# Weight conversion in a float64-weight MoE kernel: rounding the high part before the low word is added, and keeping the sum in the raw tile

## The chip, the cores and the metric

One core of one Trainium2 chip. The metric is the device time of one launch in microseconds (us). TensorE does the matmuls; VectorE, ScalarE and GpSimd do element-wise work on 128 partitions; SyncE (SP) only issues DMAs.

## The reference

Three stages in a row. The kernel's inputs are those of `setup_inputs`; the MoE weights arrive as 64-bit floats (each an `int64` bit pattern of two 32-bit words), everything else as float32.

```
attention (4 batches, 8 heads, 576 positions, head 64):
    scores = q k^T / 8 * Dmat,  Dmat = gamma_h ** (i - j) for i >= j, else 0
    x = scores @ v                                  -> 2304 tokens x 512
first MoE:   h = x @ w_in (512 x 2048);  g = (a0 + a1 h + a2 h^2 + a3 h^3)
                 / (1 + |b0||h| + |b1| h^2 + 1e-6);   x = g @ w_out
second MoE:  xn = x / sqrt(mean(x^2) + 1e-6) * rms_g
             out = (silu(xn @ w_gate) * (xn @ w_val)) @ w_out2    (512 x 1536)
```

## The kernel before

Attention runs in chunks of 128 positions (20 steps) with a running state. Both MoEs work in tiles of 384 tokens, six tiles each, features on the partitions. To keep float32 accuracy at the speed of the `fp32r` matmul format, each operand is split into a high part (rounded to fp32r) and a low part (the remainder rounded to fp32r), and each product is three matmuls: high x high, high x low, low x high. So every weight block of 128 x 512 values has to become a tile `w[:, 0]` (high) and `w[:, 1]` (low), and since the weights arrive as 64-bit floats, each must first be made a float32.

That conversion is the class `Weights`. A block goes through these steps; `hi` and `lo` are the high and the low 32-bit words of the 64-bit values, each every second word of the raw tile:

- `load` (L129): SP loads 512 KB into a `raw` tile.
- `begin`: ScalarE reads `hi` into a work tile `ft` with a scale (L141) and turns `lo` into an integer carry, in place (L142). VectorE shifts and masks `ft` (L143) and puts the sign in from `hi` (L147). GpSimd adds `lo` to `ft` as integers (L150): `ft` is then the float32 value. The next load is asked for.
- `finish`: ScalarE rounds `ft` to the high part (L156), and the engine that is passed in (VectorE or GpSimd) subtracts it from `ft` and writes the low part (L157).
- `step` does one `finish` and one `begin`, so a block is finished one step after it was begun.

`raw` has three tiles for the first MoE's weights and two for the second's; `ft` has two in both. A load needs a raw tile whose readers are done; L141 needs an `ft` tile whose readers are done.

Two instances exist. `wa` converts the 32 blocks of the first MoE during attention and the first token tile (about the first 205 us). `wb` loads two blocks then, begins its first conversions in the last token tile of the first MoE, and does most of its 36 blocks (gate, value, out for each of 12 j) in the loop over j in which the second MoE's first two token tiles are worked side by side (about 545 to 700 us). Each j of this loop has two `m2_up` (24 matmuls each: gate into bank 4, value into bank 6) and two `m2_down` (9 matmuls each), and three `step_b`: one on VectorE and two on GpSimd. `step_b` wraps the step in `tc.issue_after(mark["el"])`: its ScalarE instructions are issued behind the latest SiLU (L441). After that the remaining four token tiles need no conversion.

The order of the instructions on each engine, and of the DMAs on SP's queue, is not the order of the source: a planner puts them in order by its own estimates of when each is ready, with the source order as priority, and inserts the semaphore waits. Each engine, and SP's queue, then works strictly in that order.

Of the kernel before, what the change touches and what calls it, by code (L numbers as in the profile page):

```python
# [7 lines left out]
F32 = mybir.dt.float32  # L8
# [3 lines left out]
ACTF = mybir.ActivationFunctionType  # L12
ALU = mybir.AluOpType
# [26 lines left out]
def retention_moe_kernel(  # L40
# [19 lines left out]
    act, dve, pool, pe, sp = nc.scalar, nc.vector, nc.gpsimd, nc.tensor, nc.sync  # L60
# [55 lines left out]
    class Weights:  # L116
# [17 lines left out]
        def begin(self):  # L134
            w = self.alloc(self.n1)
            self.n1 += 1
            raw = self.raw.pop(0)
            ft = self.ft_p.tile([128, 512], I32, tag="ft", name="ft")
            f = ft.bitcast(F32)
            hi, lo = raw[:, :, 1], raw[:, :, 0]  # L140
            act.activation(out=f, in_=hi.bitcast(F32), func=ACTF.Copy, scale=2.0 ** -112)  # L141
            act.activation(out=lo, in_=lo.bitcast(U32), func=ACTF.Copy, scale=2.0 ** -29)  # L142
            dve.tensor_scalar(  # L143
                out=ft, in0=ft, scalar1=3, scalar2=0x7FFFFFFF,
                op0=ALU.logical_shift_left, op1=ALU.bitwise_and,
            )
            dve.scalar_tensor_tensor(  # L147
                out=ft, in0=hi, scalar=-0x80000000, in1=ft, op0=ALU.bitwise_and, op1=ALU.bitwise_or
            )
            pool.tensor_tensor(out=ft, in0=ft, in1=lo, op=ALU.add)  # L150
            self.mid.append((w, f))
            self.load()

        def finish(self, eng):
            w, f = self.mid.pop(0)
            act.activation(out=w[:, 0], in_=f, func=ACTF.Copy)  # L156
            eng.tensor_tensor(out=w[:, 1], in0=f, in1=w[:, 0].bitcast(F32), op=ALU.subtract)  # L157
            self.got[self.order[self.n2]] = w
            self.n2 += 1
# [367 lines left out]
    for h in range(NH - 1, -1, -1):  # L527
        pool.tensor_tensor(
            out=dmk8[:, h], in0=dmk8[:, 0], in1=gi[:, h].to_broadcast([128, CH]), op=ALU.mult
# [241 lines left out]
```

## Time and profile before

| | us |
|---|---|
| median of 3 runs | 1014.8 |
| lowest, highest | 1012.92, 1021.29 |
| profiled execution | 1015.87 |
| its span, first to last instruction | 1014.1 |
| TensorE busy | 976.3 |
| VectorE, ScalarE, GpSimd busy | 576.0, 550.8, 419.5 |
| mean granted TensorE clock (1 is full) | 0.982 |

The difference between the profiled execution and its span, 1.8 us, lies around the first and the last instruction. A busy time is the union of an engine's instructions; instructions on one engine overlap a little at their ends. "SPq" is SP's queue of DMA issues.

### The profile page before, as it was taken

How to read it: one execution, taken by the hardware profiler on the slowest of the kernel's cores; microseconds unless marked ns; L12 is line 12 of the kernel's file. 1: busy time of each engine (PE TensorE's matmuls, PEld its weight loads, DVE VectorE, ACT ScalarE, POOL GpSimd, SP SyncE). 2: the span in 40 equal slices, each digit the busy share in tenths (PEclk: the TensorE clock that was granted, in tenths of full speed). 3: DMA queues.
4: the chain of work that ended last, by engine and by line, in shares of the span. 5: the costliest groups of instructions: out<-in, count | busy, mean ns of one | idle time of the engine just before them, and what ended most of it. 6: DMA issues, size and time to landing. Idle time of an engine off the chain costs nothing.

```text
span 1014.1 us, 14962 instructions
## 1 busy us (share of the span) xinstructions
PE 976.3 (96%) x5726; PEld 912.9 (90%) x5726; DVE 576.0 (57%) x972; ACT 550.8 (54%) x1076; POOL 419.5 (41%) x379
## 2 busy tenths in 40 slices
PE   8989899889999999999989999999999999999998
PEld 6878677889999999999989989889999999999997
DVE  4999999768668677686797664444211211212211
ACT  3777676587786877878878665555212112111111
POOL 4475676574564654746647545545001001000000
PEclk7999999999999999999999999999999999999999
DMA  7848676310100100101012243333200100000000
GB/s 266 268 139 262 211 236 204 102 57 32 32 1 32 32 1 32 32 32 32 21 53 90 91 154 119 110 124 96 72 1 16 48 1 16 32 1 1 32 1 32
DMA packets 37592, 78.91 MB, mean 78 GB/s; under 512 B 5904, under 2 KB 21392, under 8 KB 37520
## 3 DMA queue, kind: packets, MB, share of 16 engines
q1 hardware_dynamic: 36512, 77.61, 23.6%
q8 instruction: 45, 0.74, 0.3%
q10 hardware_dynamic: 1008, 0.34, 0.1%
q14 instruction: 27, 0.22, 0.1%
HBM read 64.57 MB, written 13.37 MB: 77 GB/s over the span
## 4 chain that ended last, share of the span: by engine, by line
PE 58%; DVE 10%; ACT 5%; POOL 5%; DMA 4%; issue 3%; POOLq 0%; DVEq 0%; ACTq 0%
PE bank L438 7%; PE bank L436 7%; PE bank L437 7%; PE bank L308 4%; PE bank L317 4%; PE bank L318 4%; PE bank L309 4%; PE bank L310 4%; PE bank L321 4%; PE bank L454 4%; PE bank L455 4%; PE bank L453 4%; DMA raw<-in_w_val_dram 3%; POOL ft L150 3%; DVE ft L147 2%
## 5 line engine op out<-in xcount | busy, mean ns | idle before, releaser
L438 PE MATMUL bank<-x,w 128*128 128x384 f32 x528 | 177.6, 336 | 1.7 <-POOL w L157 1.7
L436 PE MATMUL bank<-x,w 128*128 128x384 f32 x528 | 177.2, 336 | 1.8 <-DVE sg L442 1.8
L437 PE MATMUL bank<-x,w 128*128 128x384 f32 x528 | 177.0, 335 | 0.0
L442 DVE TENSOR_TENSOR sg<-sg,bank 128x384 f32<-128x384 f32 x72 | 39.8, 553 | 218.6 <-PE bank L438 218.3
L150 POOL TENSOR_TENSOR ft<-ft,raw 128x512 int32<-128x512 int32 x68 | 96.1, 1413 | 120.0 <-DVE ft L147 64.2
L308 PE MATMUL bank<-x,w 128*128 128x384 f32 x384 | 131.8, 344 | 5.9 <-DVE u L346 4.8
L344 POOL TENSOR_TENSOR q<-q,ah 128x384 f32<-128x384 f32 x96 | 101.9, 1063 | 81.2 <-ACT q L340 80.7
L318 PE MATMUL bank<-g,w 128*128 128x384 f32 x384 | 126.1, 343 | 6.1 <-DVE w L157 6.1
L310 PE MATMUL bank<-x,w 128*128 128x384 f32 x384 | 131.0, 341 | 0.9 <-POOL w L157 0.6
L309 PE MATMUL bank<-x,w 128*128 128x384 f32 x384 | 130.1, 339 | 1.3 <-DVE x L212 1.3
L317 PE MATMUL bank<-g,w 128*128 128x384 f32 x384 | 126.3, 344 | 3.3 <-ACT g L364 3.3
L365 POOL TENSOR_TENSOR g<-u,g 128x384 fp32r<-128x384 f32 x96 | 100.7, 1049 | 67.0 <-issue 34.5
L441 ACT ACTIVATE sg<-bank 128x384 f32<-128x384 f32 x72 | 35.3, 490 | 147.8 <-PE bank L438 147.8
L212 POOL TENSOR_TENSOR x<-xr,x 128x384 fp32r<-128x384 f32 x44 | 46.2, 1063 | 157.8 <-ACT x L211 157.6
L436 PEld LDWEIGHTS bank<-x,w 128*128 128x128 f32 x528 | 99.2, 188 | 5.4 <-DVE sg L442 2.1
L438 PEld LDWEIGHTS bank<-x,w 128*128 128x128 f32 x528 | 99.1, 188 | 3.1 <-POOL w L157 3.0
L437 PEld LDWEIGHTS bank<-x,w 128*128 128x128 f32 x528 | 99.1, 188 | 3.0 <-POOL x L212 0.3
L444 ACT ACTIVATE y<-sg 128x384 fp32r<-128x384 f32 x72 | 37.6, 522 | 104.4 <-DVE sg L442 104.3
L345 DVE TENSOR_TENSOR u<-u,bank 128x384 f32<-128x384 f32 x96 | 52.9, 551 | 59.4 <-ACT u L341 58.8
L321 PE MATMUL bank<-g,w 128*128 128x384 f32 x384 | 86.6, 339 | 0.0
L308 PEld LDWEIGHTS bank<-x,w 128*128 128x128 f32 x384 | 73.1, 191 | 8.8 <-DVE u L346 6.2
L318 PEld LDWEIGHTS bank<-g,w 128*128 128x128 f32 x384 | 72.5, 192 | 8.8 <-DVE w L157 7.5
(98 smaller groups left out, 2080.8 us busy)
## 6 DMA issues: line engine op xcount, KB each, us to landing
raw<-in_w_out_dram SPq DMA_DIRECT2D x28, 512.0 KB, 3.5
xb<-in_qkT_dram SPq DMA_DIRECT2D x19, 512.0 KB, 4.1
kv<-in_kv_dram SPq DMA_DIRECT2D x16, 512.0 KB, 4.4
raw<-in_w_in_dram SPq DMA_DIRECT2D x16, 512.0 KB, 4.5
raw<-in_w_gate_dram SPq DMA_DIRECT2D x12, 512.0 KB, 3.5
raw<-in_w_val_dram SPq DMA_DIRECT2D x12, 512.0 KB, 3.6
xn_d<-x SPq DMA_DIRECT2D x6, 768.0 KB, 3.8
xr<-xn_d SPq DMA_DIRECT2D x24, 192.0 KB, 2.5
```

The lines of the kernel that those rows point to most:

```text
L150: pool.tensor_tensor(out=ft, in0=ft, in1=lo, op=ALU.add)
L308: pe.matmul(out=h, lhsT=w[:, 0, ks], rhs=x[:, 0, k], start=(k == 0), stop=False)
L309: pe.matmul(out=h, lhsT=w[:, 0, ks], rhs=x[:, 1, k], start=False, stop=False)
L310: pe.matmul(out=h, lhsT=w[:, 1, ks], rhs=x[:, 0, k], start=False, stop=(k == KD - 1))
L317: pe.matmul(out=acc[m], lhsT=w[:, 0, ms], rhs=g[:, 0], start=(j == 0), stop=False)
L318: pe.matmul(out=acc[m], lhsT=w[:, 1, ms], rhs=g[:, 0], start=False, stop=False)
L321: pe.matmul(out=acc[m], lhsT=w[:, 0, ms], rhs=g[:, 1], start=False, stop=(j == J1 - 1))
L344: pool.tensor_tensor(out=q, in0=q, in1=ah, op=ALU.mult)
L365: pool.tensor_tensor(out=g[:, 1], in0=u, in1=g[:, 0].bitcast(F32), op=ALU.subtract)
L436: pe.matmul(out=t, lhsT=w[:, 0, ks], rhs=x[:, 0, k], start=(k == 0), stop=False)
L437: pe.matmul(out=t, lhsT=w[:, 0, ks], rhs=x[:, 1, k], start=False, stop=False)
L438: pe.matmul(out=t, lhsT=w[:, 1, ks], rhs=x[:, 0, k], start=False, stop=(k == KD - 1))
```

## The change

The ScalarE rounding of the high part moves from `finish` to `begin`, behind the line of the GpSimd sum, and reads `ft`, which no longer gets the low word's bits. The GpSimd sum goes to `lo`, every second word of the raw tile, and the subtraction in `finish` reads it from there. The high part is then the rounding of a value that lacks the low word's carry; the low part is taken against the full sum, so that high plus low still stands for the full value.

```diff
-            pool.tensor_tensor(out=ft, in0=ft, in1=lo, op=ALU.add)
-            self.mid.append((w, f))
+            pool.tensor_tensor(out=lo, in0=ft, in1=lo, op=ALU.add)
+            act.activation(out=w[:, 0], in_=f, func=ACTF.Copy)
+            self.mid.append((w, lo.bitcast(F32)))
             self.load()
 
         def finish(self, eng):
             w, f = self.mid.pop(0)
-            act.activation(out=w[:, 0], in_=f, func=ACTF.Copy)
             eng.tensor_tensor(out=w[:, 1], in0=f, in1=w[:, 0].bitcast(F32), op=ALU.subtract)
```

## Rows read from the trace of the kernel before

**Rows 1.** The page's first part: busy us, share of the span, instructions.

```profile
PE 976.3 (96%) x5726; PEld 912.9 (90%) x5726; DVE 576.0 (57%) x972; ACT 550.8 (54%) x1076; POOL 419.5 (41%) x379
```

**Rows 2.** Busy us (instructions) of PE, PEld, DVE, ACT, POOL in two stretches; clock, DMA.

```profile
40.00:160.00 120.00, 108.92 (x878) 92.29 (x877) 118.08 (x175) 85.66 (x166) 79.18 (x62) 0.97 0.68 217
...
600.00:700.00 100.00, 97.79 (x509) 90.00 (x508) 47.33 (x83) 53.63 (x100) 50.11 (x39) 1.00 0.35 111
```

**Rows 3.** Chain of waits, 598 to 634 us: start, us, what.

```profile
604.95 3.55 DMA raw<-in_w_val_dram
...
611.67 1.31 POOL ft L150
612.98 1.26 POOL w L157
...
614.27 0.68 ACT ft L141
...
616.73 1.42 POOL ft L150
```

**Rows 4.** Timeline of SP's queue: first and last of 15 raw issues; a value load.

```profile
81.54 0.33 SPq L129 DMA_DIRECT2D raw<-in_w_in_dram  x1
...
156.88 0.33 SPq L129 DMA_DIRECT2D raw<-in_w_in_dram  x1
...
684.89 0.33 SPq L129 DMA_DIRECT2D raw<-in_w_val_dram  x1
```

**Rows 5.** Timelines of GpSimd and VectorE, second conversion: start, us, instruction, idle before.

```profile
608.45 1.32 POOL L150 TENSOR_TENSOR ft<-ft,raw 128x512 int32<-128x512 int32 x1 [3.52 <-DVE ft L147]
...
666.35 2.54 POOL L157 TENSOR_TENSOR w<-ft,w 128x512 fp32r<-128x512 f32 x2
...
618.84 0.69 DVE L157 TENSOR_TENSOR w<-ft,w 128x512 fp32r<-128x512 f32 x1 [1.87 <-ACT w L156]
```

**Rows 6.** Timeline of TensorE: starts of up, down, next up; a wait.

```profile
608.94 0.33 PE L436 MATMUL bank<-x,w 128*128 128x384 f32 x1
...
613.13 0.39 PE L453 MATMUL bank<-w,y 128*128 128x512 f32 x1
...
615.21 0.33 PE L436 MATMUL bank<-x,w 128*128 128x384 f32 x1
...
667.69 0.44 PE L438 MATMUL bank<-x,w 128*128 128x384 f32 x1 [0.41 <-POOL w L157]
```

**Rows 7.** TensorE's waits, 560 to 720 us: total, times, longest.

```profile
PE bank L438 <- POOL w L157: 1.7, 3, 1.0
```

**Rows 8.** TensorE's waits, 0 to 215 us.

```profile
PE bank L318 <- DVE w L157: 6.1, 5, 2.0
...
PE bank L308 <- ACT w L156: 1.0, 1, 1.0
```

**Rows 9.** ScalarE's waits, 0 to 215 us.

```profile
ACT ft L141 <- DVE w L157: 17.8, 12, 3.7
```

**Rows 10.** Conversion lines over the span: ns minimum/median/maximum, first and last start.

```profile
L150 POOL TENSOR_TENSOR ft<-ft,raw x68: 1288/1320/1761, 17.9 to 696.6; 128x512 int32<-128x512 int32 x68
...
L156 ACT ACTIVATE w<-ft x64: 612/630/647, 19.2 to 679.6; 128x512 fp32r<-128x512 f32 x64
...
L157 DVE TENSOR_TENSOR w<-ft,w x37: 677/693/1784, 22.1 to 672.2; 128x512 fp32r<-128x512 f32 x37
L157 POOL TENSOR_TENSOR w<-ft,w x27: 1270/1298/1732, 37.3 to 680.7; 128x512 fp32r<-128x512 f32 x27
...
L147 DVE SCALAR_TENSOR_TENSOR ft<-raw,ft x68: 674/686/1687, 17.1 to 695.6; 128x512 int32<-128x512 int32 x68
...
L143 DVE TENSOR_SCALAR ft<-ft x68: 406/428/1467, 15.2 to 694.8; 128x512 int32<-128x512 int32 x68
```

**Rows 11.** Timelines of GpSimd and VectorE: one early weight's sum and subtraction.

```profile
137.88 1.62 POOL L150 TENSOR_TENSOR ft<-ft,raw 128x512 int32<-128x512 int32 x1 [2.43 <-DMA kv<-in_kv_dram]
...
141.68 1.48 DVE L157 TENSOR_TENSOR w<-ft,w 128x512 fp32r<-128x512 f32 x1
```

## The prediction

> **What bounds the kernel now.** I read the page's busy line first: TensorE is busy 96% of the span, nothing else above 57% [rows 1]. So only TensorE's gaps are for sale, and the change touches only the weight conversion. It runs in two stretches, which the windows separate [rows 2]. In 40 to 160 us (first MoE's weights, beside attention) VectorE is busy 118.08 of 120 us and sets the pace. In 600 to 700 us (second MoE's weights) VectorE, ScalarE and GpSimd are all about half busy, TensorE 97.79 of 100. The chain of waits there does not run through TensorE but round a ring of conversion steps [rows 3]: raw load issued at 604.95, GpSimd's sum for that weight over at 611.67 + 1.31 = 612.98, a GpSimd subtraction to 614.24, the ScalarE conversion of the next weight, which that subtraction released by freeing a ft tile, its sum to 618.15, then the next load. From the value load at 604.95 to that at 684.89 [rows 3, 4] there are six rounds of three weights (gate, value, out): 79.94 / 6 = 13.32 us a round. TensorE needs 2 x (615.21 - 608.94) = 12.54 us a round [rows 6]. So the ring is the slower by 0.78 us, TensorE eats a small lead, and then waits for the low part of a weight: three waits, 1.7 us [rows 7], one at 667.69 [rows 6], just behind the gate's subtraction (666.35 + 2.54 / 2 = 667.62) [rows 5].
>
> **The change, part by part.**
> (a) The ScalarE rounding moves from finish to begin and needs the VectorE bit operations, no longer GpSimd's sum. It runs beside the sum (0.63 us against 1.32 [rows 10]), so the subtraction can follow the sum at once. In its new place ScalarE may stand through the two VectorE operations (0.43 + 0.69 = 1.1 us at the medians [rows 10]) with the SiLU and the y rounding queued behind it. ScalarE is busy 53.63 of 100 us [rows 2] and TensorE's down projection gives 615.21 - 613.13 = 2.08 us [rows 6] between reading a bank and needing it again: cost nothing; without that cover, up to 1.1 us at each of two SiLUs a round, 13 us over six rounds.
> (b) The ft tile is freed by sum and rounding instead of by the subtraction. That removes ScalarE's waits for ft: 17.8 us in 12 waits in the first stretch [rows 9], and the link at 614.27 [rows 3].
> (c) The raw tile is now freed by the subtraction, not by the sum. With two raw tiles in the second stretch, that is the ring that is left. Load issue to end of sum takes 612.98 - 604.95 = 8.03 us [rows 3]. Behind it comes the subtraction: on GpSimd directly after the sum 1.29 us, on VectorE (one weight in three) 0.77 us with its start delay [rows 5, 10]. Three weights: 3 x 8.03 + 1.29 + 1.29 + 0.77 = 27.44 us, over two tiles 13.72 us a round. That is 0.40 above 13.32; six rounds, 2.4 us later at the end.
> (d) Against that, the subtractions come sooner after their sums. Now the gate's ends 614.24 - (608.45 + 1.32) = 4.47 us after its sum, because the value's sum is queued ahead of it on GpSimd; the value's 2.52; out's 619.53 - 618.15 = 1.38 [rows 3, 5]. After: 1.29, 1.29, 0.77. TensorE uses the value's low part 12 matmuls after the gate's, 12 x 0.175 = 2.1 us later (24 in 613.13 - 608.94 [rows 6]), at 669.8; it is ready at 668.89 [rows 5], 0.9 us early, and becomes 1.23 us earlier still. So TensorE can run 2.1 us closer to the conversion. Net of this stretch: 2.4 - 2.1 = +0.3 us.
> (e) Strides. VectorE's subtraction reads every second word: the bit operation that already does so takes 686 ns against 693 contiguous [rows 10], so nothing. On GpSimd a strided read shows as 1320 against 1298 [rows 10]: +0.02. No row shows GpSimd writing with a stride; the floor is 0 (its reads stay, so no gain), the far end its slowest sum, 1761 ns, 0.44 more [rows 10]. I take 0.02, as the strided read is the nearest row; the far end adds 3 x 0.44 / 2 = 0.66 a round, 4.0 us.
> (f) SP's queue: every raw load now waits for the subtraction. In the second stretch nothing but raw loads stands behind it. In the first, attention's loads and stores do. Raw loads there come every (156.88 - 81.54) / 14 = 5.38 us [rows 4], 16.1 us for three tiles; load to sum 8.03, sum to subtraction 143.16 - 139.50 = 3.66 [rows 11], together 11.7. With 4.4 us to spare this ring does not bind: nothing, at worst the few microseconds by which attention's loads slip.
> (g) First stretch: ScalarE's ft waits go, but VectorE has the same operations and no room, so TensorE's waits there (6.1 and 1.0 us behind the conversion [rows 8]) stay. Bounds: 0 to -7; I take 0, since 118.08 of 120 is nearer to full than anything else here.
>
> Sum: the profiled execution took 1015.87 us (span 1014.1 and 1.8 around it); + 0.3 gives 1016.2. That execution is 1.07 above the median of the runs, so on the median's scale **1015 us**, and 1010 to 1021 for this case with strides, ScalarE's queue and SP's.
>
> **A rule against it.** VectorE's shift takes 428 ns at the median but up to 1467, the bit merge 686 and up to 1687 [rows 10]: VectorE loses time when GpSimd runs beside it. The Trainium skill, "SBUF — State Buffer", section "Who interferes with whom", says that a VectorE operation in a two-port mode or with two SBUF inputs and a GpSimd operation that reads SBUF exclude each other for a whole instruction; the slow rows agree in kind. It makes the third rival.
>
> **Rivals.**
> B, the subtraction stays where it is in the engines' queues. The order comes from a planner, not from this page. If GpSimd keeps the value's sum ahead of the gate's subtraction, the raw tiles are held 4.47, 2.52 and 1.38 us past the sums: (3 x 8.03 + 8.37) / 2 = 16.2 us a round, six rounds 6 x 2.9 = 17 us: 1032, more if the weights before 604.95 suffer too. It decides as soon as the mean delay from sum to end of subtraction is above 1.9 us (15 us a round, 1% of the time over six). For: that is today's order, and a load's wait then holds all loads behind it. Against: the reason for the order, a rounding that comes late on ScalarE, goes away. Chance 0.16.
> C, the ft waits did cost: their release lets the rounding chain run ahead, TensorE's 6.1 + 1.0 us [rows 8] in the first stretch and 1.7 us [rows 7] in the second vanish: 1006. For: ScalarE's ft waits stand at nearly every weight. Against: VectorE's 118.08 of 120. Chance 0.13, the part past 1% of it 0.06.
> D, exclusion. With subtraction directly behind sum, GpSimd works 2.6 us in one piece, and the other tile's shift or merge is held once per weight for the length of a subtraction, 1.27 us: (27.44 + 3.81) / 2 = 15.6 a round, + 2.3 x 6 - 2.1 = 11.7: 1027. For: the slow rows. Against: the pair at 666.35 [rows 5] already is such a piece, and its toll lies in the 8.03. Chance 0.07.
> That the change does not do what it says (rounding and sum side by side) would need ScalarE to be full; with 53.63 of 100 it is not, and I give it no chance of its own.
>
> **How the numbers follow.** No change, 1015: 0.64. The range leaves out B and the far edge of C, 0.16 and a few hundredths: 1006 to 1029. One per cent, about 10 us, is what a measurement of this kernel can tell from none. Faster by more: 0.07. Slower by more: B and most of D, 0.21. Within: 0.72.
>
> **What would show it.** Loads issued at the end of a subtraction, on SP, instead of a sum: (c). Round length between value loads near 13.7: the forecast; above 15: B or D, told apart by GpSimd's order (sum, sum, subtraction in B) and by the shift's mean (D). ScalarE without ft waits before 160 us but VectorE still full and TensorE's 40 to 160 us unchanged: (g); TensorE clearly busier there: C. A sum well above 1.32 us at its minimum: (e) wrong. SiLU waiting behind the rounding, with TensorE waiting for a bank: (a) wrong.

## The result: 0.65% slower, within the forecast of no change

| | before | after |
|---|---|---|
| median, us (13 runs each) | 1014.85 | 1021.31 |
| lowest to highest, us | 1009.91 to 1021.29 | 1018.93 to 1027.91 |
| ratio after / before, 95% interval | | 1.0065 [1.0048, 1.0083] |
| profiled execution, us | 1015.87 | 1022.4 |
| its span, us; granted TensorE clock | 1014.1; 0.982 | 1020.6; 0.974 |

The time lies within the range (1006 to 1029), and the loss is under the 1% that the forecast called no change. It is a loss all the same, 6.5 us, where the sum of terms gave +0.3. In the changed kernel's lines L150 is the sum (now into `raw`), L151 the rounding and L157 the subtraction.

The page's busy line, against [rows 1]: TensorE is busy 3.4 us longer, VectorE and ScalarE slightly less, GpSimd 5.7 us longer.

```profile
PE 979.7 (96%) x5726; PEld 920.3 (90%) x5726; DVE 574.7 (56%) x972; ACT 549.2 (54%) x1076; POOL 425.2 (42%) x379
```

The two stretches of [rows 2] (same columns). From 600 to 700 us TensorE is now busy throughout, at a lower granted clock; from 40 to 160 us the trace has 51 fewer matmuls than before (827 against 878), at 0.95 instead of 0.97, and VectorE is still nearly full.

```profile
40.00:160.00 120.00, 106.90 (x827) 93.24 (x826) 116.17 (x167) 85.79 (x169) 80.48 (x60) 0.95 0.62 203
600.00:700.00 100.00, 100.00 (x515) 93.80 (x514) 50.19 (x89) 55.98 (x101) 53.53 (x39) 0.97 0.41 129
```

**The second conversion does what the change promises.** Timelines of SP, GpSimd and VectorE in its steady part (start, us, instruction, idle before), against [rows 3 to 5]:

```profile
615.35 0.33 SPq L129 DMA_DIRECT2D raw<-in_w_val_dram  x1
...
621.80 1.50 POOL L150 TENSOR_TENSOR raw<-ft,raw 128x512 int32<-128x512 int32 x1 [1.14 <-issue]
623.37 1.32 POOL L157 TENSOR_TENSOR w<-raw,w 128x512 fp32r<-128x512 f32 x1
626.18 1.51 POOL L150 TENSOR_TENSOR raw<-ft,raw 128x512 int32<-128x512 int32 x1 [1.49 <-DVE ft L147]
...
627.72 0.69 DVE L157 TENSOR_TENSOR w<-raw,w 128x512 fp32r<-128x512 f32 x1 [1.21 <-POOL raw L150]
...
690.55 0.33 SPq L129 DMA_DIRECT2D raw<-in_w_val_dram  x1
```

The subtraction follows its sum at once: the value's sum ends at 621.80 + 1.50 = 623.30, its subtraction at 624.69, and a load (the gate's) is issued at 624.72. From value load to value load there are again six rounds: (690.55 - 615.35) / 6 = 12.53 us a round, TensorE's own pace (12.54) and no longer the ring's (13.32). No TensorE wait for a low part is left; those of [rows 7] are gone. TensorE's waits from 545 to 720 us (total, times, longest) are others:

```profile
PE bank L436 <- ACT sg L441: 4.7, 2, 2.8
PE bank L436 <- DVE u L346: 0.7, 1, 0.7
```

**It pays at the switch to the second MoE.** ScalarE's timeline at those two waits:

```profile
551.34 0.63 ACT L151 ACTIVATE w<-ft 128x512 fp32r<-128x512 f32 x1 [0.33 <-DVE ft L147]
551.99 1.28 ACT L441 ACT_TABLE_LOAD   x1
553.28 0.49 ACT L441 ACTIVATE sg<-bank 128x384 f32<-128x384 f32 x1
...
594.67 0.66 ACT L141 ACTIVATE ft<-raw 128x512 f32<-128x512 f32 x1 [2.55 <-DMA raw<-in_w_out_dram]
...
596.90 0.63 ACT L151 ACTIVATE w<-ft 128x512 fp32r<-128x512 f32 x1 [0.99 <-DVE ft L147]
597.54 1.28 ACT L441 ACT_TABLE_LOAD   x1
598.84 0.49 ACT L441 ACTIVATE sg<-bank 128x384 f32<-128x384 f32 x1
```

A SiLU stands behind a rounding, which stands behind VectorE's merge, and at 594.67 behind a raw load that could be issued only after a subtraction. TensorE waits 1.91 us up to 553.83 and 2.76 us up to 599.38, and the granted clock drops at each wait, to the lower of its two levels for 3.4 and 6.8 us (windows, columns as in [rows 2]):

```profile
553.00:560.00 7.00, 6.17 (x26) 6.17 (x27) 2.85 (x4) 5.51 (x10) 7.00 (x7) 0.76 0.45 126
598.00:606.00 8.00, 6.62 (x22) 6.62 (x23) 5.03 (x9) 4.01 (x7) 3.27 (x3) 0.57 0.51 164
```

**Where the 6.5 us arise.** I set the same instructions of both traces side by side, after minus before. The 17th evaluation of the first MoE (about 204 us) starts 3.9 us late; the lag is 2.4 to 4.7 us for the next 20 evaluations and 3.7 us in most of those after them, to about 530 us; at the seventh SiLU (589.5 us before) it is 9.4, at the tenth 11.0; it falls back to 6.2 at the 24th, since the conversion now keeps up, and stays at 6.6. In these two executions, then, some 3.7 us belong to the first conversion and the rest to the switch less the gain. Two single executions do not size this; the experiments weigh the two halves with many runs.

### The profile page after: what moved, and what is told of

The parts are those of the page before. It is cut to its first block, busy times and chain, and to the rows that moved or that the text cites. A ratio compares the mean times of both kernels' runs of the same rounds, so it can differ in the third digit from the quotient of the medians.

```text
span 1020.6 us, 15004 instructions
## 1 busy us (share of the span) xinstructions
PE 979.7 (96%) x5726; PEld 920.3 (90%) x5726; DVE 574.7 (56%) x972; ACT 549.2 (54%) x1076; POOL 425.2 (42%) x379
## 3 DMA queue, kind: packets, MB, share of 16 engines
q10 hardware_dynamic: 1008, 0.34, 0.1%
## 4 chain that ended last, share of the span: by engine, by line
PE 70%; DVE 6%; ACT 3%; POOL 2%; DMA 2%; issue 2%; DVEq 0%; ACTq 0%; POOLq 0%
PE bank L436 9%; PE bank L438 9%; PE bank L437 9%; PE bank L308 5%; PE bank L321 5%; PE bank L317 5%; PE bank L310 5%; PE bank L318 5%; PE bank L309 5%; PE bank L454 5%; PE bank L455 5%; PE bank L453 5%; DMA raw<-in_w_val_dram 1%; DVE x L417 1%; POOL w L157 1%
## 5 line engine op out<-in xcount | busy, mean ns | idle before, releaser
L150 POOL TENSOR_TENSOR raw<-ft,raw 128x512 int32<-128x512 int32 x68 | 99.1, 1458 | 99.3 <-DVE ft L147 64.7
L436 PEld LDWEIGHTS bank<-x,w 128*128 128x128 f32 x528 | 100.5, 190 | 9.1 <-ACT sg L441 5.3
L437 PEld LDWEIGHTS bank<-x,w 128*128 128x128 f32 x528 | 100.3, 190 | 2.8
L438 PEld LDWEIGHTS bank<-x,w 128*128 128x128 f32 x528 | 100.1, 190 | 0.1
L308 PEld LDWEIGHTS bank<-x,w 128*128 128x128 f32 x384 | 74.2, 193 | 9.8 <-DVE u L346 7.4
L310 PEld LDWEIGHTS bank<-x,w 128*128 128x128 f32 x384 | 74.4, 194 | 4.7 <-DVE w L157 4.1
```

Of the source, the lines that this page charges most:

```text
L150: pool.tensor_tensor(out=lo, in0=ft, in1=lo, op=ALU.add)
L308: pe.matmul(out=h, lhsT=w[:, 0, ks], rhs=x[:, 0, k], start=(k == 0), stop=False)
L310: pe.matmul(out=h, lhsT=w[:, 1, ks], rhs=x[:, 0, k], start=False, stop=(k == KD - 1))
L436: pe.matmul(out=t, lhsT=w[:, 0, ks], rhs=x[:, 0, k], start=(k == 0), stop=False)
L437: pe.matmul(out=t, lhsT=w[:, 0, ks], rhs=x[:, 1, k], start=False, stop=False)
L438: pe.matmul(out=t, lhsT=w[:, 1, ks], rhs=x[:, 0, k], start=False, stop=(k == KD - 1))
```

## The experiments

All ratios are to the kernel before on the same chip, with 95% intervals. Each expectation names the theories as they stood when it was written.

### Which half of the change, and which part

The change in the first conversion alone (`if self.order is not order:` keeps the old code for `wb`), and in the second alone:

> The change in the first MoE's conversion alone; the second MoE's is as before. Theory T (the loss lies in two places: 3.7 us by the end of the first conversion, 2.8 us net at the switch to the second MoE): +3.7 us, ratio 1.0037, all of it there by 205 us, and nothing lost or won after it. Rival R (the ring of raw tiles: only two tiles are too few, three have slack): no loss, 1.000. Rival P (any new order by the planner costs or gives a few us, here and there): anything within 0.7%, and what the two half changes cost does not add up to the whole.

> The change in the second MoE's conversion alone. Theory T: +2.8 us, ratio 1.0028: TensorE waits some 4.7 us in two stalls behind the first SiLU and the seventh, each followed by a stretch at half clock, about 6 us lost by the seventh SiLU; then the conversion keeps up (rounds near 12.6 us, no wait for a low part) and 3 to 4 us come back. Rival R: rounds longer than 13.3 us and longer waits for low parts, all of the 6.5 us here, 1.0065. Rival P: not 1.0065 less what the other half costs.

Measured: first only 1021.35 us, 1.0062 [1.0041, 1.0082], the whole loss; second only 1014.25, 0.9988 [0.9968, 1.0008], nothing. Theory T's sizes (1.0037 and 1.0028) and rival R's (1.000 and 1.0065) both missed. The cut is clean: up to 500 us ScalarE, VectorE and GpSimd work in the changed kernel's order in the first kernel, and in the order of before in the second. The second's trace has the same waits at the switch (TensorE's waits, 540 to 720 us; L447 is its SiLU), but here without any time at the lower clock level (1.00 over this stretch):

```profile
PE bank L442 <- ACT sg L447: 4.8, 3, 2.4
```

Its seventh SiLU is 5.1 us late and its 24th 0.4 us early: the stall is real, and by the 24th it is made up for, as the conversion keeps up. So the loss is to be sought in the first conversion, where only waits for weights had been looked at.

The two ideas of the change, one at a time, in both conversions. Early rounding, with the sum back in `ft` (against the kernel before; the rounding in `finish` goes):

```diff
+            act.activation(out=w[:, 0], in_=f, func=ACTF.Copy)
             pool.tensor_tensor(out=ft, in0=ft, in1=lo, op=ALU.add)
```

> Both conversions: the rounding early (in begin, ahead of the sum), but the sum back in the ft tile, so that the sum waits for the rounding and the raw tile is free after the sum. Leaves out the low word in the high part as the change does. Theory T: the stall behind the first SiLU comes from the rounding's place and stays (1.9 us and about 1.7 us of half clock), the one behind the seventh comes from a raw load that waits for a subtraction and goes; the first conversion as before: ratio 1.002 to 1.004. Rival R: the raw tiles are free as before, so 1.000.

And the sum in the raw tile, with the rounding left in `finish` (against the changed kernel):

```diff
             pool.tensor_tensor(out=lo, in0=ft, in1=lo, op=ALU.add)
-            act.activation(out=w[:, 0], in_=f, func=ACTF.Copy)
-            self.mid.append((w, lo.bitcast(F32)))
+            self.mid.append((w, lo.bitcast(F32), f))
...
-            w, f = self.mid.pop(0)
+            w, f, f0 = self.mid.pop(0)
+            act.activation(out=w[:, 0], in_=f0, func=ACTF.Copy)
```

> Both conversions: the sum in the raw tile as in the change, but the rounding (of the value without the low word) back in finish, so it comes a step later. Theory T: no stall behind the first SiLU, but loads late: the first conversion's 3.7 us and a stall at the seventh SiLU stay: 1.003 to 1.006. Rival R: the raw tile is held even longer than in the change (the subtraction waits for the late rounding), rounds near 16 us, 15 us or more lost: above 1.012.

Measured: early rounding 1012.93 us, 0.9974 [0.9951, 0.9996]; sum in raw 1023.89, 1.0082 [1.0051, 1.0113]. The early rounding gains about 2.6 us; the sum's new place costs 8 to 9 us. Neither theory had these sizes: T expected 1.002 to 1.004 and 1.003 to 1.006, R 1.000 and above 1.012.

### What of the sum's new place

With the sum in `raw`, the subtraction no longer reads `ft`, so an `ft` tile comes free earlier. Laid side by side, the traces differ in VectorE's order: attention's outputs (L245, into `gx`) come behind more of the conversion's work. VectorE's subtractions of low parts (L157) up to the start of the 15th of 20 attention outputs, by windows of that line (stretch, length, busy us (count), then clock, DMA share, GB/s). Before, at 153.2 us:

```profile
0.00:153.20 153.20, 19.00 (x18) 0.93 0.70 232
```

After, at 169.7:

```profile
0.00:169.60 169.60, 21.57 (x21) 0.90 0.63 215
```

In the changed kernel three more weights are finished ahead of that output, and it comes 16.4 us later. Theory Q: the wait for an `ft` tile, which [rows 9] show as ScalarE's loss, also kept the conversion from being ordered ahead of attention; without it the planner puts conversion and first MoE before attention on VectorE, and the end of the stretch, which needs attention, comes late. Rival L: the held raw tile delays the loads (or the strided write costs).

Q can be tried without the change: the kernel before with three `ft` tiles. The space comes from one of attention's three `ret` tiles, so the kernel before with two `ret` tiles is its control. And the opposite, the changed kernel with two raw tiles, holds the conversion back again (it also asks for two raw loads at the start, not three):

```diff
-    ft_p = s_ctx.enter_context(tc.tile_pool(name="ft", bufs=2, side="right"))
+    ft_p = s_ctx.enter_context(tc.tile_pool(name="ft", bufs=3, side="right"))
...
-    ret_p = s_ctx.enter_context(tc.tile_pool(name="ret", bufs=3, side="right"))
+    ret_p = s_ctx.enter_context(tc.tile_pool(name="ret", bufs=2, side="right"))
```

> The kernel before with a third ft tile in the first conversion (a ret tile of the attention is given up for the room; the next kernel is the control for that). Nothing of the change is in it: late rounding, sum in ft, raw tile free after the sum. Theory Q (the ft ring held the conversion back; without that wait the planner lets conversion and MoE run ahead of the attention on VectorE, and the attention's last chunks, with the five blocks that need its buffers, are left over as a serial tail): its queue order runs ahead like the changed kernel's, so +5 to +6.5 us against the control, ratio about 1.006, lost by 205 us. Rival L (the raw tile held for the subtraction makes loads late and the weights with them): loads are asked for as before, so 1.000 or faster, since ScalarE's 20 us of waits for ft go.

> The kernel before with two ret tiles instead of three, the control for the third ft tile. The order of VectorE's queue is that of the kernel before in every chunk looked at. Both theories: within 0.2% of before.

```diff
-    raw_p = s_ctx.enter_context(tc.tile_pool(name="raw", bufs=3, side="right"))
+    raw_p = s_ctx.enter_context(tc.tile_pool(name="raw", bufs=2, side="right"))
```

> The changed kernel with two raw tiles instead of three in the first conversion. Loads come later still, and the conversion is held back: at the 15th of 20 chunks of the attention VectorE's queue has 15 of its subtractions ahead of the attention's step, where the changed kernel has 21 and the kernel before 18. Theory Q: the run-ahead is gone, so most of the loss goes too: 1.000 to 1.003, unless the weights now come so late that TensorE waits for them. Rival L: worse than the change, above 1.0065, with longer waits of TensorE for weights.

Measured: three `ft` tiles 1035.89 us, 1.0196 [1.0158, 1.0233]; control 1023.16, 1.0082 [1.0056, 1.0109]. The control's expectation failed: the lost `ret` tile costs 0.8%, and its profiled execution (1017.11 us, well below its median) doesn't show where. Against the control, the `ft` tile costs 12.7 us, with Q's sign and twice its 5 to 6.5 us. The count, for three `ft` tiles, up to its 15th output at 176.7 us:

```profile
0.00:176.70 176.70, 19.29 (x21) 0.88 0.65 212
```

and for the control, at 154.9 us, as many as before:

```profile
0.00:154.90 154.90, 19.91 (x18) 0.97 0.71 230
```

So a third work tile, which leaves the conversion's instructions and its loads as they were, makes a slower kernel, with the conversion as far ahead at the 15th output as in the changed kernel (further at the 13th: 20 subtractions against 17, 15 before) and nothing else of the change. Two raw tiles gave 1030.75, 1.0145 [1.0099, 1.0191], a miss for Q's number: the conversion was held back too far (15 subtractions ahead of the 15th output; the 24th subtraction, counted over both engines, 27 us late), and ScalarE waits for its loads. ScalarE's waits there, 0 to 215 us:

```profile
ACT ft L141 <- DMA raw<-in_w_out_dram: 14.1, 8, 5.4
...
ACT ft L141 <- DMA raw<-in_w_in_dram: 11.6, 9, 3.7
```

L is real with two tiles, but a ring is the wrong tool to tell the theories apart: it moves the loads as well. What was missing was the change, whole, with an explicit edge that holds the order:

```diff
-        dve.tensor_tensor(out=xo, in0=o[:, :, 0:n], in1=gq[:, :, 0:n], op=ALU.mult)
+        mark["at"] = dve.tensor_tensor(out=xo, in0=o[:, :, 0:n], in1=gq[:, :, 0:n], op=ALU.mult)
...
-            wa.step(dve if wa.n1 % 4 else pool)
+            with tc.issue_after(mark["at"].ins):
+                wa.step(dve if wa.n1 % 4 else pool)
```

> The change whole, with one addition: the first conversion's steps are put on VectorE behind the latest attention output (the multiplication into gx), so that the conversion can't run ahead of attention. In its queue order the 15th attention chunk's output stands behind 12 split passes of the first MoE and 17 subtractions of low parts (before: 13 and 18; the change: 15 and 21). Theory Q (the change lost its time because, without the wait for a work tile, conversion and first MoE are ordered ahead of attention on VectorE): ratio to the kernel before 0.996 to 1.001, and attention's 13th and 19th chunk end within 4 us of their times in the kernel before. Rival L (the sum in the raw tile itself costs: the strided write, or loads that come later since the raw tile is held): the ratio stays at 1.005 to 1.009, whatever the order. If the holding back goes too far, as with two raw tiles, ratio over 1.008 and the 16th subtraction over 8 us late.

Measured: 1008.55 us, 0.9935 [0.991, 0.9961]; against the change's 1.0065 that is 0.9935 / 1.0065 = 0.987. Strided write, held raw tiles and early free `ft` tiles are all still there, and the loss is gone, as Q said and L did not. Its 15th output comes at 148.3 us:

```profile
0.00:148.20 148.20, 16.72 (x17) 0.91 0.67 227
```

Attention's 13th and 19th outputs come 3.0 and 4.1 us earlier than before, and the 17th evaluation of the MoE 5.1 us earlier. The expectation had the sign; the size is better than its 0.996.

Two things limit this. The kernel before with the same edge was not run, so how much of the 0.9935 is the change's and how much the edge's is not shown, nor whether L still costs something that the edge makes up for. And the edge, though written at the first conversion, also moved the planner's order at the switch: between 500 and 600 us about 50 instructions of ScalarE and as many of VectorE stand elsewhere than in the changed kernel. In the profiled execution the lead over the kernel before is 5.1 us at the 17th evaluation, 1.1 at the 80th, 0.9 at the first SiLU and 6.4 at the 24th, so most of it is won around the switch and behind it. TensorE waits less for SiLUs there than in the changed kernel (540 to 720 us; 4.7 there):

```profile
PE bank L436 <- ACT sg L441: 2.0, 2, 1.7
```

and the granted clock stays up (545 to 720 us, the changed kernel and then this one):

```profile
545.00:720.00 175.00, 169.65 (x874) 158.99 (x873) 90.51 (x149) 101.68 (x182) 94.47 (x72) 0.97 0.36 114
545.00:720.00 175.00, 172.04 (x901) 159.70 (x900) 90.65 (x146) 94.12 (x171) 90.80 (x68) 1.00 0.37 118
```

Over the kernels run up to here, subtractions on VectorE ahead of the 15th attention output:

| kernel | subtractions | 15th output, us | ratio |
|---|---|---|---|
| before | 18 | 153.2 | 1 |
| change | 21 | 169.7 | 1.0065 |
| change, first conversion only | 21 | 169.2 | 1.0062 |
| sum in raw only | 21 | 172.6 | 1.0082 |
| before, 3 `ft`, 2 `ret` | 21 | 176.7 | 1.0196 |
| before, 2 `ret` | 18 | 154.9 | 1.0082 |
| change, second conversion only | 18 | 154.2 | 0.9988 |
| early rounding only | 18 | 152.9 | 0.9974 |
| change, order held | 17 | 148.3 | 0.9935 |
| change, 2 raw | 15 | 146.7 | 1.0145 |

All four kernels with 21 have a late 15th output and lose 0.6% or more. A smaller count is no promise: the control with 18 loses 0.8%, and 15 is too few.

### A version that beats both

The mixed version: first conversion with early rounding and the sum in `ft`; second conversion as in the change, with a third raw tile (the final output tiles are taken from that pool, which makes the room) and the two roundings at the switch put behind the first SiLU.

```diff
-            raw_b = new_pool("rawb", 2, "right")
+            raw_b = new_pool("rawb", 3, "right")
...
-                ob = o_p.tile([128, DM], F32, tag="ob", name="ob")
+                ob = raw_b.tile([128, 512, 2], I32, tag="raw", name="raw")
+                ob = ob.rearrange("p a b -> p (a b)").bitcast(F32)[:, 0:DM]
...
+    with tc.issue_after(mark["el"].ins):
+        wb.round()
...
-    wb.step(dve)
+    with tc.issue_after(mark["el"].ins):
+        wb.step(dve)
```

> A candidate. First conversion: rounding early, but the sum back in ft (that gave 0.9974 in both conversions). Second conversion: the change's flow, a third raw tile (the output tiles share the raw tiles' room), and the roundings of the two blocks at the switch queued behind the first SiLU. Theory Q and the two stalls at the switch: first stretch as before or 1 to 2 us better, no stall of TensorE behind the first and the seventh SiLU (3 to 5 us in the kernel with the change in the second conversion alone), no wait for a low part: 1006 to 1010 us, ratio 0.992 to 0.996. Rival P (any new order gives or takes a few us): anything from 0.994 to 1.004.

Without the third raw tile, and without the moved roundings:

> The mixed version without the third raw tile: early rounding with the sum in the work tile in the first conversion; the change's flow in the second, with the roundings at the change of MoE put behind the first SiLU. If the mixed version's gain in the second conversion is the roundings' place, ratio 0.991 to 0.995. If it is the third raw tile, 0.996 to 0.999, as the early rounding alone (0.9974).

> The mixed version with the third raw tile but with the roundings where the change puts them. If the gain of the mixed version in the second conversion is the third raw tile, ratio 0.991 to 0.995, and TensorE's wait for the first SiLUs of the second MoE shorter than 2.5 us. If it is the roundings' place, 0.996 to 0.999, and that wait over 4 us as in the change (4.7).

And the mixed version's second conversion on top of the change with its order held:

> The kernel of the run before this one, and in the second conversion what the mixed version has: a third raw tile there, with the output tiles taken from that pool, and the two roundings at the change of MoE put behind the first SiLU. The sum is in the raw tile in both conversions. Theory Q: both parts add up, ratio 0.990 to 0.995, the same as the mixed version within 0.3%. Rival L: 0.998 to 1.004.

| kernel | us | ratio |
|---|---|---|
| mixed | 1007.85 | 0.9923 [0.9892, 0.9954] |
| mixed, no third raw tile | 1011.63 | 0.9975 [0.9956, 0.9993] |
| mixed, roundings not moved | 1006.31 | 0.9939 [0.9911, 0.9967] |
| change, order held, with the mixed second conversion | 1002.91 | 0.9884 [0.986, 0.9908] |

The third raw tile is what helps: without it 0.9975, the same as the early rounding alone (0.9974). Moving the roundings shows no gain beyond the intervals. TensorE's waits from 540 to 720 us point the same way, in one execution each. Without the third tile, roundings moved (L452 is its SiLU):

```profile
PE bank L447 <- ACT sg L452: 2.8, 1, 2.8
```

With it, roundings not moved:

```profile
PE bank L441 <- DVE sg L447: 0.9, 1, 0.9
PE bank L441 <- ACT sg L446: 0.9, 1, 0.9
```

Without the third tile the SiLU was held up by a rounding whose weight had come late (ScalarE waits 1.98 us for it, up to 582.21). With two raw tiles ScalarE waits 12.6 and 12.1 us for raw loads from 545 to 720 us (out and value weights in the changed kernel), and in the last version of the table, with three, it waits for none of these loads. The last version keeps all of the change, with the order held and the third tile. It is the fastest here, 1.16% below the kernel before, and its expectation (0.990 to 0.995, within 0.3% of the mixed version) was too careful.

## Why the prediction was right, and where it was wrong

- **The time (1015, no change).** Right: 0.65% more, inside the range and under the 1% that was called no change. The mechanism was right for the second conversion's flow only. The first conversion, put at 0 in (g), cost 6.3 us by the run of that half, and no term or rival led to this loss; that it stayed under 1% is luck. The 0 of the second conversion came from other terms than the forecast's: a stall at the switch, and a conversion that then keeps up.
- **(a) ScalarE's queue, costed nothing.** Wrong at the switch. "TensorE's down projection gives 2.08 us" holds in the steady part, where no SiLU wait is left; at the change of MoE a table load of 1.28 us stands between rounding and SiLU as well, and TensorE waited 4.7 us, with 10.2 us at the lower clock level. The far end (1.1 us at each SiLU of the steady rounds) had the right mechanism in the wrong place: two SiLUs, 1.9 and 2.8 us, and none of the steady ones.
- **(b) the ft waits go.** Right: L141's waits for a subtraction are gone from ScalarE's list in the first stretch. But ScalarE gains no time by it: what it then waits for is the merge, at the rounding:

```profile
ACT w L151 <- DVE ft L147: 19.9, 14, 4.1
```

- **(c) the raw ring, 13.72 us a round.** Mis-sized. Loads are issued at the end of the subtraction, as said. But the 8.03 us from load to end of sum, taken for all three weights, was the value's alone: between 604 and 691 us the medians before are 8.02 (value), 8.82 (out) and 9.46 (gate), of which 0.7 to 2.3 us lie between the load's landing and L141. After, that gap is 0.1 us and the medians are 7.29, 7.02 and 6.92 (the 7.95 from 615.35 to 623.30 above is one of the longer ones). With the subtractions, (7.29 + 7.02 + 6.92 + 1.39 + 1.39 + 0.72) / 2 = 12.4 us a round, no more than TensorE's 12.54; the round measured 12.53.
- **(d) subtractions sooner.** Right: the value's ends 1.39 us after its sum (forecast 1.29), out's 628.41 - 627.69 = 0.72 (0.77); rival B's order (sum, sum, subtraction) did not come. The 2.4 us of (c) did not either, so the second conversion gains about what the switch costs: 0.9988.
- **(e) strides, +0.02 us a sum.** The sum's median went from 1320 ns [rows 10] to 1496 over the span, inside the bounds (0 to 0.44), nearer the middle:

```profile
L150 POOL TENSOR_TENSOR raw<-ft,raw x68: 1293/1496/1756, 17.1 to 701.9; 128x512 int32<-128x512 int32 x68
```

  The minimum did not move (1288 to 1293), 25 of the 68 take 1337 ns or less, and a kernel with the same sums (median 1489) runs at 0.9935: 0.18 us at a sum did not decide.
- **(f) SP's queue, 4.4 us to spare.** Wrong in its sizes, without harm that shows. The 8.03 us from load to sum came from the second stretch; for the loads issued from 75 to 160 us the median is 15.4 before and 13.2 after. With 2.9 us to the end of the subtraction the changed kernel holds a tile 16.1 us, and three loads come in 15.8, so the ring has nothing to spare. The loads still come every 5.3 us (5.4 before). ScalarE waits 13.5 us for raw loads in the first 215 us, against 8.0 before; with the order held it waits 13.8, and that kernel is fast. Attention's loads do slip: GpSimd's scaling of the keys (L187) waits for them, 0.3 us in one wait before, and after:

```profile
POOL kv L187 <- DMA kv<-in_kv_dram: 6.9, 3, 3.5
```

  TensorE's wait behind that scaling does not grow (1.8 us before, 1.3 after).
- **(g) the first stretch, gain 0 because VectorE is full.** This is the step that failed. VectorE's busy share was read as a limit, but what mattered was which work VectorE did first. Before, the `ft` ring ordered it; with the ring gone the order changed to the bad, 6.3 us by the run of that half alone. With the order held, VectorE is busy 111.39 of 120 us there, against 118.08 [rows 2], and the 17th evaluation comes 5.1 us early, of which 1.1 are left at the 80th:

```profile
40.00:160.00 120.00, 108.79 (x866) 93.45 (x864) 111.39 (x172) 82.47 (x161) 77.11 (x60) 0.94 0.66 217
```

- **Rival C (1006 us, chance 0.13).** It did not come, and the kernel with the order held reaches about its time (0.9935 x 1014.85 = 1008 us) by another path: TensorE's waits for low parts in the first 215 us do not vanish there (6.1 us at this line before [rows 8]):

```profile
PE bank L318 <- DVE w L157: 6.6, 3, 4.0
```

- **Rival D, exclusion.** The Trainium skill ("SBUF — State Buffer", "Who interferes with whom") has VectorE held by GpSimd; the trace agrees in kind. The shift's median in the first 215 us rises from 424 to 647 ns in the changed kernel:

```profile
L143 DVE TENSOR_SCALAR ft<-ft x32: 407/647/1531, 14.3 to 199.0; 128x512 int32<-128x512 int32 x32
```

  With the order held, the same instructions with the same subtractions and sums take 418:

```profile
L143 DVE TENSOR_SCALAR ft<-ft x32: 409/418/1454, 14.6 to 201.4; 128x512 int32<-128x512 int32 x32
```

  So the toll depends on what lies beside what: of the 32 shifts, 14 take over 450 ns before, 19 after and 12 with the order held, and every one of these starts while a GpSimd instruction is running. It is at most 32 x 0.23 = 7 us of VectorE's time, much of it given back by other lines: VectorE's busy time to 205 us is 181.42 against 179.80. The second conversion, where D put its price, does not show it: from 600 to 705 us the shift's median is 428 ns before and after.

**What stays open.** Why the planner puts the conversion ahead when `ft` comes free early was not traced inside it; that it does is shown by the third `ft` tile. How much of the loss is VectorE's order itself and how much the granted clock was not separated. The time at the lower level in the profiled executions is about 36 us before, 53 after and 31 with the order held. Over many executions, span x (1 - mean granted clock) estimates what that level takes: its median is 16.7 us for the kernel before (26 executions, beside the first four experiments), 16.2 with the second conversion alone and 16.1 with the order held, but 23.4 for the change and 24.0 with the first conversion alone. The 6.7 us between 16.7 and 23.4 are as much as the whole loss; whether the clock is how the late order costs time, or goes along with it, is not shown. Executions of one kernel differ by several us, so single traces place a loss but do not size it: the early rounding's trace, the slowest of its 12 executions, has the 17th evaluation 5.3 us late with only 18 subtractions ahead of the 15th output. The 0.8% of the `ret` tile is unexplained.

## What to carry to other kernels

A wait in a list of waits may be holding an order in place: before taking it away, ask which work the engines will then do sooner, and whose work stands behind that on the fullest engine. If freeing a buffer makes a kernel slower, try to hold the order with an explicit edge rather than by giving the buffer back: here the same change went from +0.65% to -0.65%. Run the edge on the old kernel too, which was not done here. When a tile's life is lengthened, count the tiles of that ring again; one more raw tile was worth 0.4 to 0.5% in the second conversion.

## What the runs showed of the hardware

- In the changed kernel a TensorE wait of 1.9 us was followed by 3.4 us, and one of 2.8 us came with 6.8 us, at the lower of the two clock levels (granted 0.76 and 0.57 in the windows above), so a short stall can cost more than its own length. It need not: with the change in the second conversion alone, waits of 1.9 and 2.4 us at the same places left the granted clock at 1.00.
- GpSimd's sum with a strided write has the minimum of the contiguous one (1293 against 1288 ns) but a median of 1496 against 1320. What makes the longer ones longer was not found.
- VectorE's shift took 406 to 429 ns in 51 of the 96 cases in the first 215 us of three traces (before, after, order held), and up to 1531 ns in the rest. All 45 slow ones started while a GpSimd instruction was running, and 8 of the quick ones.
- ScalarE's table load before the SiLU takes 1.28 us and starts behind the rounding (551.97 to 551.99), so a late rounding delays the SiLU by itself and leaves the load still to come.
